# Eight half blocks of early gate/up products for nine, and one more Strassen unit in the FFN

## The chip, the cores and the metric

The kernel runs on one core of a Trainium2 chip. A core has TensorE (PE, matmuls; PEld is its weight load), VectorE (DVE), ScalarE (ACT), GpSimd (POOL), SyncE (SP, which here only issues DMAs) and 16 DMA engines. Engines run their own instruction streams in order and meet through semaphores. The metric is the device time of one execution in microseconds (us); the number for a kernel is the median of several runs.

## The reference

Two parts share one layer-normalised input `xn` (2048 tokens, D = 576): a linear attention with a softmax feature map (32 heads of 18), and a SwiGLU FFN with F = 4608 that gates its output. All numbers are float32.

```python
xn = _layernorm(x)
# attention
q, k, v = split_heads(xn @ wqkv)
pq = einsum("bhsd,hdf->bhsf", q, w_phi)            # same for k
phi_q = concat([softmax(pq), softmax(-pq)])        # same for k
kv = einsum("bhsf,bhsd->bhfd", phi_k, v); z = phi_k.sum(tokens)
o = (phi_q @ kv) / (phi_q @ z + 1e-6)
s = merge_heads(o) @ wo
# FFN
g = silu((silu(xn @ w_gate) * (xn @ w_up)) @ w_down)
return x + s * g
```

## The kernel before, in words

**Precision.** Each float32 operand is split into a high part that TensorE reads exactly (`hi`, a cast on ScalarE) and the rest (`lo`, a subtraction on VectorE), and a product is made of three: hi·hi, hi·lo and lo·hi (`split`, L72). A full product over D = 576 of 128 rows of weights with 512 tokens is 14 matmuls (`xw`, L98).

**Stages.** The attention comes first: layer norm, keys and values, then the 16 q tiles of 128 tokens (`q_tile`, L823). For each pair of q tiles the softmax is done on VectorE (`softmax_parts`, L525: max and min, a subtraction, two exps on ScalarE into two halves of `e`, then the sum; L832 to L842: denominators and scaling of `e`). One pair later `numer` (L845) takes five groups of heads: four transposes into `pt` (L854), cast `ph` and subtraction `pl`, six products with the key-value sums (L861), again cast `oh` and subtraction `ol`; `pt`, `ph` and `pl` have two buffers each. The last group's low part goes through SP (`lo`, `km`). `project` (L872) multiplies with `wo` (14 matmuls for each of four halves, L889), and ScalarE copies the result out (`so` or `e`, L895).

**Early products.** The FFN works on 36 blocks of 128 of F and on two halves of 1024 tokens (i = 0 and 1). For the first blocks the gate and up products are made during the attention (`early_weights`, `early_tile`, L127 and L141): for a half block two token quarters of 512, each 14 matmuls for gate, a silu on ScalarE, 14 matmuls for up, and a product on VectorE; the result `h` goes to DRAM (`h_dram`). `EARLY` = 4 and `FIRST` = (5, 4) say that half 0 has blocks 0 to 4 early and half 1 blocks 0 to 3, nine half blocks. They are written behind the attention in the code, and the scheduler puts their matmuls (`pe`) where the attention leaves PE free. Block 4 of half 0 is the last, written after the rest (L1464 to L1469).

**FFN units.** A later block of a half is a unit of `gate_up` (L1034): gate and up of both quarters in seven products instead of eight (Strassen), 7 matmuls each (`product`, L1010), into `px`, `py`, `pw` and, in the first two units, a `pd` bank. Its weights come from `gate_up_weights` (L958): in half 0, and for blocks under `FIRST[0]` in half 1, from the raw weights `ld`, with four sums on POOL (`ts`, `ld`), four casts, four subtractions (tiles `w`), and a store of the parts in `w_dram` for half 1, which otherwise only loads them. The last 64 of the 576 rows come as "tails" (`wt`), which `tails` (L805) prepares in DRAM during the attention for four blocks at a time: a load, four POOL subtractions, a cast, a subtraction and twelve POOL DMAs. The first units' weights may not start before one of the last projection's copies (L1471, `outs[-3]`).

An early block is in its half a stored unit, which only loads `h`. `units` (L1419) is the order of blocks in each half; stored blocks stand at every fourth place of the beginning, and block 4 of half 1 in the middle. Behind each pair of units the down products (L1136, into `pd`) are queued and drawn a few at a time between the products of the units by `fill` (L1452): four times in a unit of `gate_up`, twice in a stored one.

What sets the order on each engine is the scheduler's list, fixed when the program is built: an instruction that waits holds all behind it on its engine.

Of the kernel before, what the change touches and what calls it, by code (L numbers as in the profile page):

```python
# [23 lines left out]
NF = F // P  # L24
# [5 lines left out]
NL = GROUPS[-1][1]  # L30
NK = NL + NL // 2
QS = 256
EARLY = 4
FIRST = (EARLY + 1, EARLY)
TAILS = (NF - EARLY + 3) // 4
LAG = 3
SHORT = range(22, NF - 5, 4)
# [24 lines left out]
def gated_hedgehog_kernel(ctx: ExitStack, tc, x, w_qk, w_v, consts_in, wo, w_gu, w_tail, w_down, out):  # L62
# [5 lines left out]
    nc = tc.nc  # L68
# [7 lines left out]
    def split_rows(hi, lo, src):  # L76
        nc.scalar.copy(hi, src)
        nc.vector.tensor_sub(lo, src[:, :, 0:2], hi[:, :, 0:2])
        nc.vector.tensor_sub(hi[64:96, :, 2], src[64:96, :, 2], hi[64:96, :, 2])
# [6 lines left out]
    s_dram = dram.tile([S, D], F32, name="s_dram")  # L86
    h_dram = dram.tile([2, FIRST[0], P, HS], F32, name="h_dram")
    x_dram = dram.tile([2, 4, P, 4, P], F32, name="x_dram")
    sum_dram = dram.tile([2, P, 4, 4, 5, P], F32, name="sum_dram")
    w_dram = dram.tile([NF - EARLY, P, 7, 4, P], F32, name="w_dram")  # L90
    t_dram = dram.tile([TAILS, 4, 3, 32, 7, P], F32, name="t_dram")
# [6 lines left out]
    def xw(ps, i, j, cols, wh, wl, stationary_x):  # L98
        pairs = []
        for k in range(2):  # L100
            b = XB[i][2 * j + k]
            for c in range(2):
                pairs += [(b[:, c, cols], w[:, k, c]) for w in (wh, wl)]
                pairs += [(b[:, 3 + c, cols], wh[:, k, c])]
            pairs += [(b[:, 2, cols], wh[:, k, 2])]
        for n, (a, b) in enumerate(pairs):
            l, r = (a, b) if stationary_x else (b, a)
            last = nc.tensor.matmul(ps, l, r, start=n == 0, stop=n == len(pairs) - 1)  # L108
        return last
# [9 lines left out]
    def early_raw_part(f, m):  # L119
        raw = epool.tile([P, 2, 3, P], F32, name="raw", bufs=2)  # L120
        nc.sync.dma_start(raw, w_gu[f, :, m:m + 2])
        return raw

    def early_place():
        return epool.tile([P, 2, 3, P], F32R, name="wh", bufs=3), epool.tile([P, 2, 2, P], F32R, name="wl", bufs=3)

    def early_weights(f, *behind):  # L127
        parts = []
        for m in (0, 2):
            raw = early_raw_part(f, m)  # L130
            parts.append(early_place())
            with ExitStack() as order:
                for b in behind:
                    order.enter_context(tc.issue_after(b.ins))
                with tc.high_priority():
                    split_rows(*parts[-1], raw)
        return parts
# [3 lines left out]
    def early_tile(f, i, parts, js=(0, 1), banks=None, store=nc.sync, behind=None):  # L141
        for j in js:
            pg, pu = banks or [eps.tile([P, BT], F32, name="pe") for _ in range(2)]
            xw(pg, i, j, slice(0, BT), *parts[0], False)
            h = epool.tile([P, BT], F32, name="h")
            with tc.high_priority():
                silus.append(nc.scalar.activation(h, pg, AF.Silu))
            last = xw(pu, i, j, slice(0, BT), *parts[1], False)
            with tc.issue_after(behind.ins) if behind else ExitStack():
                with tc.high_priority():  # L150
                    nc.vector.tensor_mul(h, pu, h)
            store.dma_start(h_dram[i, f, :, j * BT:(j + 1) * BT], h)
        return last

    outs = []
    with ExitStack() as att:
# [18 lines left out]
        with ExitStack() as wst:  # L175
# [4 lines left out]
            with ExitStack() as pst:  # L180
# [15 lines left out]
                xns, ws, wv, halves = {}, {}, {}, {}  # L196
# [485 lines left out]
            order = [6, 7, 0, 1, 2, 3, 4, 5]  # L682
# [101 lines left out]
        with ExitStack() as qst:  # L784
# [113 lines left out]
            order = list(range(S // QS // 2, S // QS)) + list(range(S // QS // 2))  # L898
# [13 lines left out]
                with tc.issue_after(last_e[3 * n // 2 + 2].ins):  # L912
                    tails(n, exps[NT + 3 * n // 2 + 2])

        for f, halves in [(1, (0,)), (0, (0,))] + [(f, (1, 0)) for f in range(2, EARLY)]:
            parts = first_weights.pop() if f == 1 else early_weights(
                f, *{0: read[2 * NT + 1:2 * NT + 2], 2: (read[2 * NT + 3], exps[NT + 1])}.get(f, ()))
            for i in halves:
                early_tile(f, i, parts, (1,) if f == 1 else (0, 1), behind=read[2 * NT + 1] if f == 1 else None)
# [8 lines left out]
    def operands(i):  # L928

        xo = [None] * 7  # L930
        for n in (0, 6, 3, 1, 5, 4, 2):
            if n < 3:
                j = (0, 1, 3)[n]
                if i:
                    t = xpool.tile([P, 5, BT], F32R, name=f"X0{j}")
                    nc.sync.dma_start(t.bitcast(F32), a_dram[n])
                else:
                    t = XB[0][j]
                xo[n] = [t[:, c] for c in range(5)]
                continue  # L940
            j = n - 3
            t = xpool.tile([P, 5, BT], F32R, name=f"X1{j}")
            parts = 1 if i else 4
            rows = t.bitcast(F32).rearrange("p c n -> p (c n)").rearrange("p (a m) -> p a m", a=parts)
            src = sum_dram[i, :, j].rearrange("p s c n -> p (s c n)").rearrange("p (a m) -> p a m", a=parts)
            for a in range(parts):
                nc.sync.dma_start(rows[:, a], src[:, a])
            v = t.rearrange("p c n -> p (c n)").rearrange("p (s c n) -> p s c n", s=4, c=5)
            xo[n] = [v[:, :, c] for c in range(5)]
        return xo  # L950

    def raw_weights(f):
        ld = fw.tile([P, 2, D], F32, name="ld", bufs=2).rearrange("p a b -> p (a b)")
        ld = ld[:, 0:8 * P].rearrange("p (m c n) -> p m c n", m=4, c=2)
        nc.sync.dma_start(ld, w_gu[f, :, :, 0:2])
        return ld

    def gate_up_weights(i, f, ld=None):  # L958

        parts, wt = {}, wts[0]  # L960
        wts.reverse()
        n, q = divmod(f - EARLY, 4)
        raw = i == 0 or f < FIRST[0]
        if raw:
# [3 lines left out]
        def ready(m, src):  # L968
            k = 1 if m == 6 else 2
            w = fw.tile([P, k, 4, P], F32R, name=f"w{k}", bufs=2 if k == 1 else 4)  # L970
            if not raw:
                nc.sync.dma_start(w.bitcast(F32), w_dram[f - EARLY, :, m:m + k])
            else:
                split(w[:, :, 0:2], w[:, :, 2:4], src)
                if i == 0 and f < NF - 1:
                    nc.sync.dma_start(w_dram[f - EARLY, :, m:m + k], w.bitcast(F32))
            for c in range(k):
                parts[m + c] = w[:, c]
# [11 lines left out]
        else:  # L990
            ready(2, ld[:, 2:4] if raw else None)
        held = {0: silus[-2:-1], 2: tops[0:1], 3: tops[1:2]}.get(f - FIRST[0]) if i == 0 else None

        def last(held=held):
            with tc.issue_after(held[0].ins) if held else ExitStack():
                ready(6, ld[:, 1:2] if raw else None)
# [3 lines left out]
        elif i == 0 and f in SHORT:  # L1000
            later.append(lambda: last(copies[-1:]))
        elif (i, f) == (0, FIRST[0] + 3):
            opened.append(lambda: ready(6, ld[:, 1:2]))
# [416 lines left out]
    for i in range(2):  # L1420
        order = [NF - 1] * i + list(range(FIRST[0], NF - i))
        if i:
            order.insert(NF // 2, EARLY)
        for f in range(FIRST[i]):
            order.insert(4 * f + 1 - i, f)
        units += [(i, n, f) for n, f in enumerate(order)]
# [34 lines left out]

    todo = [(i, f) for i, n, f in units if f >= FIRST[i] and (i == 0 or f < NF - 1)]
    kept = []
    parts = early_weights(EARLY)  # L1464
    first_rows = [acc[:, 1].rearrange("p (a b) n -> p a (b n)", a=2)[:, n] for n in range(2)]
    for t, f in zip(first_rows, (FIRST[0], 0)):
        nc.sync.dma_start(t, w_down[f * P:(f + 1) * P, :])
    xo = operands(0)
    early_tile(EARLY, 0, parts, store=nc.gpsimd)  # L1469
    early_raw = [raw_weights(f) for _, f in todo[0:2]]  # L1470
    with tc.issue_after(outs[-3].ins):  # L1471
        ready = [gate_up_weights(*todo.pop(0), early_raw.pop(0))]
# [84 lines left out]
```

## Time and profile before

| | us |
|---|---|
| median of 3 runs | 1579.47 (1579.38 to 1579.89) |
| profiled execution | 1580.98 |
| its span, first to last instruction | 1579.2 |
| attention with the q tiles, from the first early matmul at L108 to the last projection | 219.9 to 456.8 |
| first matmul of the FFN units (L1051) | 467.70 |

The profile is of one execution. A group's row gives the busy time and the mean of one instruction; matmuls overlap in PE's pipeline, so the distance between two starts, not the record's length, tells what one costs. The chain of waits is followed back from the last instruction, so it tells which engine's work sets the end. The rows that matter are shown in the prediction.

### The profile page before, as it was taken

The page shows a single profiled execution, that of the slowest core. Times are in us where ns is not written, and L with a number is a line of the kernel's source. Part 1 is how long each engine was busy: PE and PEld are TensorE (multiplying, and loading weights), DVE is VectorE, ACT ScalarE, POOL GpSimd, SP SyncE. Part 2 cuts the span into 40 slices and gives each one's busy share as a digit, 9 for nine tenths or more (in the row PEclk, how much of TensorE's full clock was granted, in tenths as well). Part 3 has the DMA queues.
Part 4 walks back from the last instruction along what each step waited for, and adds up shares of the span by engine and source line. Part 5 has one row for each costly group of instructions (what it writes and reads, how often), then busy time and mean ns, then how long its engine had stood idle before and what let it go on. Part 6 is the DMA issues. An engine that isn't in the chain of part 4 may idle for free.

```text
span 1579.2 us, 25305 instructions
## 1 busy us (share of the span) xinstructions
PE 1570.4 (99%) x9371; PEld 1415.5 (90%) x9371; DVE 1162.8 (74%) x1722; ACT 729.0 (46%) x1408; POOL 671.5 (43%) x723
## 2 busy tenths in 40 slices
PE   9999999999999999999999999999999999999998
PEld 7999999999988898898888888888888888888887
DVE  7777769999947787987777778545766667666577
ACT  6633344545445644444544444454333343333334
POOL 5766653334125545563644444313323324133133
PEclk9999999999999999999999999999999999999999
DMA  9424343336357455454545543964545655555445
GB/s 284 142 67 165 135 154 117 105 118 209 120 185 259 159 181 198 161 182 174 186 161 202 177 168 125 355 210 139 155 146 157 193 173 161 175 184 187 145 118 182
DMA packets 123287, 269.05 MB, mean 170 GB/s; under 512 B 12436, under 2 KB 54100, under 8 KB 121884
## 3 DMA queue, kind: packets, MB, share of 16 engines
q1 hardware_dynamic: 110572, 246.57, 47.6%
q0 software_dynamic: 3552, 12.59, 2.8%
q10 hardware_dynamic: 9040, 8.28, 1.6%
q8 instruction: 74, 1.21, 0.3%
q14 instruction: 49, 0.40, 0.1%
HBM read 167.54 MB, written 99.09 MB: 169 GB/s over the span
## 4 chain that ended last, share of the span: by engine, by line
PE 96%; POOL 1%; DVE 1%; DMA 1%; issue 1%; ACT 0%; SPq 0%; DVEq 0%; POOLq 0%; ACTq 0%
PE px L1014 25%; PE pd L1136 25%; PE pw L1014 12%; PE p L108 6%; PE py L1014 6%; PE pe L108 5%; PE p L889 4%; PE kvp L547 2%; PE pt L861 2%; PE pe L50 1%; PE vx L636 1%; PE pt L854 1%; PE tp L50 1%; PE vw L636 1%; DMA wst<-in_A_w_qk 0%
## 5 line engine op out<-in xcount | busy, mean ns | idle before, releaser
L1136 PEld LDWEIGHTS pd<-dw,hh 128*128 128x128 f32 x3000 | 421.8, 188 | 19.8 <-DVE acc L1372 0.8
L1136 PE MATMUL pd<-dw,hh 128*128 128x288 f32 x3000 | 435.7, 294 | 0.0
L1014 PE MATMUL px<-X,w 128*128 128x512 f32 x1512 | 385.6, 390 | 0.0
L1014 PEld LDWEIGHTS px<-X,w 128*128 128x128 f32 x1512 | 274.6, 188 | 46.1
L1014 PE MATMUL pw<-X,w 128*128 128x512 f32 x744 | 188.8, 389 | 0.0
L1014 PEld LDWEIGHTS pw<-X,w 128*128 128x128 f32 x744 | 139.5, 188 | 28.9
L1372 DVE TENSOR_TENSOR acc<-pd,acc 128x576 f32<-128x576 f32 x128 | 96.4, 753 | 93.3 <-PE pd L1136 92.6
L1047 DVE TENSOR_TENSOR s<-pw,s 128x512 f32<-128x512 f32 x126 | 86.4, 687 | 89.5 <-ACT s L1042 78.9
L1042 ACT COPY s<-px 128x512 f32<-128x512 f32 x126 | 73.6, 584 | 144.9 <-PE px L1014 144.7
L73 ACT CAST hh<-ha 128x512 fp32r<-128x512 f32 x139 | 82.2, 620 | 94.2 <-PE pd L1136 68.7
L74 DVE TENSOR_TENSOR hh<-ha,hh 128x512 fp32r<-128x512 f32 x139 | 111.8, 829 | 18.8 <-ACT hh L73 18.5
L1344 POOL TENSOR_TENSOR hb<-hb 128x512 f32<-128x512 f32 x34 | 46.6, 1372 | 157.2 <-DVE hb L1059 156.8
L74 DVE TENSOR_TENSOR w<-ld,w 128x512 fp32r<-128x512 f32 (+1 forms) x96 | 76.9, 803 | 38.6 <-ACT w L73 37.7
L1014 PE MATMUL px<-X,wt 128*128 128x512 f32 x252 | 98.0, 389 | 0.0
L1014 PE MATMUL py<-X,w 128*128 128x512 f32 x378 | 96.5, 390 | 0.0
L1357 POOL TENSOR_TENSOR ha<-ha 128x512 f32<-128x512 f32 x34 | 52.3, 1554 | 100.1 <-DVE hh L74 94.7
L1331 POOL TENSOR_TENSOR h<-ha,hb 128x512 f32<-128x512 f32 x34 | 44.5, 1309 | 107.2 <-DVE ha L1063 76.4
L983 POOL TENSOR_TENSOR ts<-ld 128x256 f32<-128x256 f32 x32 | 26.8, 839 | 139.6 <-issue 67.4
L73 ACT CAST w<-ld 128x512 fp32r<-128x512 f32 (+1 forms) x96 | 52.7, 550 | 70.3 <-POOL ld L986 40.6
L1067 ACT COPY py<-px 128x512 f32<-128x512 f32 x63 | 36.0, 572 | 106.1 <-PE px L1014 94.6
L108 PE MATMUL pe<-X,wh 128*128 128x512 f32 x260 | 80.4, 395 | 0.0
L1014 PEld LDWEIGHTS py<-X,w 128*128 128x128 f32 x378 | 68.3, 188 | 10.8
(325 smaller groups left out, 3242.3 us busy)
## 6 DMA issues: line engine op xcount, KB each, us to landing
w_dram<-w SPq DMA_DIRECT2D x90, 512.0 KB, 2.6
w<-w_dram SPq DMA_DIRECT2D x90, 512.0 KB, 4.3
wt<-t_dram SPq DMA_DIRECT2D x62, 336.0 KB, 4.4
ld<-in_B_w_gu SPq DMA_DIRECT2D x32, 512.0 KB, 6.3
rt<-in_B_w_down SPq DMA_DIRECT2D x33, 288.0 KB, 5.1
rb<-in_B_w_down SPq DMA_DIRECT2D x33, 288.0 KB, 3.3
w_dram<-w SPq DMA_DIRECT2D x30, 256.0 KB, 2.1
w<-w_dram SPq DMA_DIRECT2D x30, 256.0 KB, 2.7
```

What stands on the lines that cost most here:

```text
L73: cast = nc.scalar.copy(hi, src)
L74: return cast, nc.vector.tensor_sub(lo, src, hi)
L108: last = nc.tensor.matmul(ps, l, r, start=n == 0, stop=n == len(pairs) - 1)
L889: nc.tensor.matmul(ps[:, 0:HALF], a, bw, start=k == 0, stop=k == len(mm) - 1)
L1014: nc.tensor.matmul(ps, l, r, start=first and n == 0, stop=last and n == len(mm) - 1, skip_group_check=True)
L1042: snaps.append(nc.scalar.copy(t, ps))
L1047: nc.vector.tensor_add(t, ps, t)
L1136: nc.tensor.matmul(ps, l, r, start=first and n == 0 and m == 0, stop=n == len(hs) - 1 and m == 2, skip_group_check=True)
L1331: sub(s, g["h"][0][0], g["h"][0][1])
L1344: nc.gpsimd.tensor_add(a21, a21, g["h"][1][1])
L1357: sub(a12, a12, g["h"][0][0])
L1372: adds.append(nc.vector.tensor_add(a2, pd[:, :, 0:HALF], a2))
```

## The change

`EARLY` becomes 3 and `FIRST` (5, 3). Half 0 keeps blocks 0 to 4 early. Half 1 keeps only 0 to 2; its block 3 becomes a unit of `gate_up` with raw weights, placed in the middle of the half, and block 4 four places behind it. The early list loses one half block of 56 matmuls (block 3, half 1). `TAILS` goes from 8 to 9, as there are now 33 blocks from `EARLY` on.

```diff
-EARLY = 4
-FIRST = (EARLY + 1, EARLY)
+EARLY = 3
+FIRST = (EARLY + 2, EARLY)
 TAILS = (NF - EARLY + 3) // 4
...
-        for f, halves in [(1, (0,)), (0, (0,))] + [(f, (1, 0)) for f in range(2, EARLY)]:
+        for f, halves in [(1, (0,)), (0, (0,))] + [(f, (1, 0)) for f in range(2, EARLY)] + [(EARLY, (0,))]:
...
         if i:
-            order.insert(NF // 2, EARLY)
+            for f in range(EARLY, FIRST[0]):
+                order.insert(NF // 2 + 4 * (f - EARLY), f)
...
-    parts = early_weights(EARLY)
+    parts = early_weights(FIRST[0] - 1)
...
-    early_tile(EARLY, 0, parts, store=nc.gpsimd)
+    early_tile(FIRST[0] - 1, 0, parts, store=nc.gpsimd)
```

The order of instructions moves at the end of the attention. Up to the 14th q tile PE's order is the same. Three places follow, each as it stood before and as it stands now.

The first is ScalarE around the exps of the last q tile (`e`). Before, the table of the silu (L147) is not loaded between the last tile's two exps:

```order
L73 CAST ph<-pt 126x512 x2
L534 ACT_TABLE_LOAD
L534 ACTIVATE e<-e 128x576
L73 CAST oh<-pt 126x256 x2
L73 CAST ph<-pt 126x512
L534 ACTIVATE e<-e 128x576
L73 CAST oh<-pt 126x256
L895 COPY so<-p 128x288
```

Now a silu stands between them, with two table loads, and the copy of a projection too:

```order
L73 CAST ph<-pt 126x512 x2
L73 CAST oh<-pt 126x256 x2
L73 CAST ph<-pt 126x512
L534 ACTIVATE e<-e 128x576
L147 ACT_TABLE_LOAD
L147 ACTIVATE h<-pe 128x512
L73 CAST oh<-pt 126x256
L895 COPY so<-p 128x288
L534 ACT_TABLE_LOAD
L534 ACTIVATE e<-e 128x576
```

The second exp of the last tile moved behind that silu, the copy and both loads.

The second place is PE in the last pair's `numer`, around the products of the first two groups (72 and 126 rows). Before:

```order
L861 MATMUL pt<-ph,KVH 72x256 x2
L861 MATMUL pt<-ph,KVL 72x256 x2
L861 MATMUL pt<-pl,KVH 72x256 x2
L108 MATMUL pe<-X_694,wh 128x512
L108 MATMUL pe<-X_695,wh 128x512
L108 MATMUL pe<-X_695,wl 128x512
L108 MATMUL pe<-X_695,wh 128x512 x2
```

Now, with the end of the last early block (`pe`) in front:

```order
L108 MATMUL pe<-X_695,wl 128x512
L108 MATMUL pe<-X_695,wh 128x512 x2
L854 MATMUL pt<-consts,e 72x128 x3
L854 MATMUL pt<-consts,e 126x128 x3
L861 MATMUL pt<-ph,KVH 72x256 x2
L861 MATMUL pt<-ph,KVL 72x256 x2
L861 MATMUL pt<-pl,KVH 72x256 x2
L861 MATMUL pt<-ph,KVH 126x256 x2
```

All early matmuls now stand ahead of the last tile's transposes, and none between or behind the steps of the last `numer`.

The third is PE at the start of the FFN's units (`w` and `wt` are the weights and their tails, `X` the token sums). Before:

```order
L108 MATMUL pe<-X_695,wl 128x512
L108 MATMUL pe<-X_695,wh 128x512 x2
L1051 MATMUL py<-X_588,w_5275 128x512
L1014 MATMUL px<-X_588,w_5275 128x512 x6
L1014 MATMUL px<-X_588,wt_5162 128x512
L1014 MATMUL pw<-X_5182,w_5284 128x512 x6
L1014 MATMUL pw<-X_5182,wt_5162 128x512
```

Now:

```order
L889 MATMUL p_4548<-WOH,km 128x288
L889 MATMUL p_4548<-WOL,km 128x288
L1051 MATMUL py<-X_588,w_5228 128x512
L1014 MATMUL px<-X_588,w_5228 128x512 x6
L1014 MATMUL pw<-X_5135,w_5237 128x512 x6
L1014 MATMUL pd<-X_5150,w_5241 128x512 x5
L1014 MATMUL px<-X_588,wt_5115 128x512
L1014 MATMUL pw<-X_5135,wt_5115 128x512
```

The units now follow the last projection (L889) at once, and the first three products are begun with all but their tails before the first `wt` is read.

## The prediction

> **What bounds the kernel now.** I read the page's engine shares first, then the chain of work that ended last, then the busy time by stretches.
>
> ```profile
> PE 1570.4 (99%) x9371; PEld 1415.5 (90%) x9371; DVE 1162.8 (74%) x1722; ACT 729.0 (46%) x1408; POOL 671.5 (43%) x723
> PE 96%; POOL 1%; DVE 1%; DMA 1%; issue 1%; ACT 0%; SPq 0%; DVEq 0%; POOLq 0%; ACTq 0%
> 390.00:420.00 30.00, 30.00 (x212) 28.58 (x211) 27.87 (x41) 14.13 (x25) 6.24 (x13) 1.00 0.55 166
> 420.00:450.00 30.00, 30.00 (x199) 26.92 (x198) 22.36 (x41) 14.78 (x27) 0.44 (x1) 1.00 0.23 77
> 450.00:480.00 30.00, 30.00 (x151) 25.50 (x150) 14.64 (x21) 11.43 (x24) 13.79 (x19) 1.00 0.75 253
> 1170.00:1490.00 320.00, 320.00 (x1753) 283.47 (x1753) 208.66 (x300) 119.69 (x236) 100.72 (x84) 1.00 0.56 171
> ```
>
> In the windows the columns are length, busy time of PE, PEld, DVE, ACT and POOL, clock, DMA share and GB/s. TensorE never stops: 96% of the chain is PE, and no stretch quoted shows it idle. So the time is a sum of matmul slots, and any new wait of PE is added in full. But near 400 us VectorE is nearly as full (27.87 of 30). There PE stays busy because early products of the FFN (`pe`) stand between the attention's own. I look for what happens when some are taken out.
>
> The length of a slot comes from runs of equal matmuls in the chain view (start, length, what):
>
> ```profile
> 241.08 13.40 PE pe L108 x59
> 266.18 7.44 PE p L889 x56
> 456.98 10.89 PE pe L108 x48
> 477.61 3.17 PE px L1014 x14
> 437.02 1.04 PE L854 MATMUL pt<-consts,e 128*72 128x128 f32 x8
> 437.82 0.70 PE L108 MATMUL pe<-X,wh 128*128 128x512 f32 x2
> 439.52 0.40 PE L861 MATMUL pt<-ph,KVH 72*72 72x256 f32 x2
> 439.99 0.40 PE L861 MATMUL pt<-pl,KVH 72*72 72x256 f32 x2
> 440.23 0.62 PE L108 MATMUL pe<-X,wh 128*128 128x512 f32 x2
> ```
>
> A 512-wide matmul takes 0.227 us (13.40/59, 10.89/48, 3.17/14), a 288-wide one 0.133 us (7.44/56). The last five rows are of the timeline: eight transposes take 0.1 us each (437.02 to 437.82), six products of L861 0.118 each (439.52 to 440.23). A record's own length overlaps its neighbours and isn't used.
>
> **The count.** One early half block goes: 2 token quarters x gate and up x 14 matmuls = 56, or 12.7 us. It becomes a unit of `gate_up`: 7 products x 7 = 49, or 11.1 us. The down products stay. Net **-1.6 us** (7 x 0.227).
>
> ```profile
> 458.88 0.61 ACT L73 CAST w<-ld 128x512 fp32r<-128x512 f32 x1
> 459.52 0.69 DVE L74 TENSOR_TENSOR w<-ld,w 128x512 fp32r<-128x512 f32 x1 [6.59 <-ACT w L73]
> L816 DVE TENSOR_TENSOR tl<-tl,th x8: 1081/1083/1084, 269.2 to 407.4; 128x896 f32<-128x896 f32 x8
> ```
>
> The new unit stands in the second FFN half, with weights read raw, as block 4 has there already. VectorE is busy 208.66 of 320 us in that stretch and PE 320 of 320, so its casts, subtractions and loads lie beside matmuls. Cost 0; if that cover were gone, four casts of 0.61 and four subtractions of 0.69, 5.2 us.
>
> The ninth tail group costs VectorE and ScalarE one instruction each, POOL four and twelve DMA issues.
> VectorE's 1.1 us stand just before the last softmax sum, where VectorE waits for ScalarE anyway (below). Cost 0, at most 1.1. POOL is busy 0.44 of the 30 us from 420.
>
> **Where the fillers are missing.** PE's order is the same up to the 14th of the 16 q tiles. From the last q tile on, 38 early matmuls are left for 98 before, and none behind the last softmax, where 71 stood. These waits follow.
>
> ```profile
> 418.40 0.39 PE L108 MATMUL pe<-X,wh 128*128 128x512 f32 x1
> 423.21 1.28 ACT L534 ACT_TABLE_LOAD   x1
> 424.51 0.69 ACT L534 ACTIVATE e<-e 128x576 f32<-128x576 f32 x1
> 429.89 1.35 DVE L538 TENSOR_REDUCE sm<-e 128x64 f32<-128x1152 f32 x1
> 432.43 0.40 ACT L895 COPY so<-p 128x288 f32<-128x288 f32 x1 [2.28 <-PE p L889]
> 435.62 1.36 DVE L842 TENSOR_TENSOR e<-e,y 128x1152 f32<-128x1152 f32 x1
> 436.89 0.29 PE L889 MATMUL p<-WOL,km 108*128 108x288 f32 x1
> 445.25 0.37 ACT L73 CAST oh<-pt 126x256 fp32r<-126x256 f32 x1 [1.00 <-PE pt L861]
> 445.65 0.42 DVE L74 TENSOR_TENSOR ol<-pt,oh 126x256 fp32r<-126x256 f32 x1 [0.68 <-ACT oh L73]
> ```
>
> *Last softmax.* Before, PE comes to the last transposes (437.02) just as VectorE ends the scaling of the last e (435.62 + 1.36). Now PE does 15 more early matmuls ahead of that point (4 before the last q product ends, 11 behind), +3.4 us: 440.4. VectorE's side: ScalarE now loads the Silu table, computes a silu, and loads the Exp table back between the two exps of the last tile. The silu needs PE to have gone 24 early matmuls, 24 of L861 and 12 transposes beyond the last q product, which ended at 418.40 (the first `pe` behind it) and now ends 0.9 later, 419.3: 5.4 + 2.8 + 1.2, so 428.7. Behind it stands a copy of `p`, ready after 17 projections: 428.7 + 2 early matmuls (0.5) + 6 of L861 (0.7) + 2.3 + 0.3 (the last one's length) = 432.5. Copy 0.4, table 1.3, exp 0.7: 434.9, and some 0.1 between engines, 435.0. From the sum to the end of the scaling took 436.98 - 429.89 = 7.1 us, with one oh/ol subtraction (0.4) that now comes earlier, so 6.7: 441.7. PE waits 441.7 - 440.4 = **1.3 us**. Bounds: 0, if that tail of ScalarE is quicker by it, and 2.6, two table loads in full.
>
> [...]
>
> *Last head groups.* Behind the transposes each of five groups goes PE, ScalarE cast, VectorE subtraction, PE, cast, subtraction, with two buffers of `pt`.
>
> ```profile
> 438.02 0.58 ACT L73 CAST ph<-pt 72x512 fp32r<-72x512 f32 x1 [0.40 <-PE pt L854]
> 438.63 0.69 DVE L74 TENSOR_TENSOR pl<-pt,ph 72x512 fp32r<-72x512 f32 x1 [1.65 <-ACT ph L73]
> 456.68 0.29 PE L889 MATMUL p<-WOL,km 108*128 108x288 f32 x1
> ```
>
> The stretch from 437.02 to 456.81 is 19.8 us: 20 transposes, 30 of L861, 56 projections and 23 early matmuls make 2.0 + 3.5 + 7.4 + 5.2 = 18.1, so 1.7 us of waiting are there already. Without the 23, and with two transposes done earlier, the work is 12.7. Going through the new order with cast 0.58, subtraction 0.69, short cast 0.37 and short subtraction 0.42, PE waits 1.3 us for the first group, 0.65 for the buffer of the second, 0.4, 0.2 and 0.3 for the next, 0.65 for the last `oh`: 3.5 us. New: 3.5 - 1.7 = **1.8 us**. Bounds: 0, and 5.2 (every early matmul there turned into waiting).
>
> *Opening of the FFN.* Before, 48 early matmuls (10.9 us) cover the splitting of the first weights, which stands behind the last projection's copies on ScalarE. Now the FFN follows at once.
>
> ```profile
> 457.01 0.40 ACT L895 COPY e<-p 128x288 f32<-128x288 f32 x1 [1.37 <-PE p L889]
> 457.44 0.36 ACTq L896 DMA_DIRECT2D s_dram<-e  x1
> 460.61 0.43 SPq L981 DMA_DIRECT2D wt<-t_dram  x1
> 467.70 0.39 PE L1051 MATMUL py<-X,w 128*128 128x512 f32 x1
> wt<-t_dram SPq DMA_DIRECT2D x62, 336.0 KB, 4.4
> rt<-in_B_w_down SPq DMA_DIRECT2D x33, 288.0 KB, 5.1
> ld<-in_B_w_gu SPq DMA_DIRECT2D x32, 512.0 KB, 6.3
> ```
>
> Let E be the end of the projections (456.81 before). The copy starts at E+0.2, its DMA is issued by E+1.0, the cast of `w` ends at E+1.6, and the first matmul comes at E+1.7: wait 1.7. The low part ends at E+2.35, 0.3 after PE wants it. Then 18 matmuls run to E+6.1. The tail rows `wt` are issued 0.4 behind the low part and land 4.4 us later, E+7.15: wait 1.0. The copy of `px` stands on ScalarE behind a cast of `dw`, whose rows (issued E+0.25, 5.1 to land) and POOL's work on them hold it to about E+8.5, 0.3 beyond PE. A table load (1.28) ahead of the first silu makes about 0.2 more. Sum **3.5 us**. Bounds: 1.7 (the cast alone) and 10.9 (nothing starts earlier than now). I keep near the rows of the chain, since each link has one.
>
> Sum: -1.6 + 1.3 + 1.8 + 3.5 = **+5.0 us**. On the profiled execution (1580.98, span 1579.2) that is 1586.0, span 1584.2; on the median of the runs, 1579.47, it is **1584.5 us**, 0.3% slower. 0.2% (3.2 us) is about what a measurement of this kernel can tell from no change.
>
> **Rivals.** (1) *Not slower, small waits.* PE and VectorE are level at 436.9 now; if ScalarE fits its table loads into the 3.4 us by which PE comes later, the softmax wait is 0, and the chain behind it then runs on free engines. With 0, 0.5 and 2.5: +1.4, 1580.9. It decides at waits of 4.8 us in all, below which the change can't be told from none. For it: ACT is half idle there (14.78 of 30). Against: the order of ACT is fixed, and each of its links has a row.
> (2) *The count alone:* no wait, 1577.9. Against: the first cast can't start before the projections' copies end.
> (3) *Queue heads.* On SP the load of the third weights (`ld`, 6.3 us) now stands behind the stores of the second unit's parts. The last of these needs a buffer that PE frees with the first unit's `py` group (E+8.5 and 14 matmuls, E+11.7), then a cast and a subtraction (1.3) and its stores: the load goes at about E+13.8 and lands at E+20; ScalarE's cast waiting for it blocks copies that release PE, which wants them from E+21 on. If it, or the `dw` rows, land 3 us later: 1587.5.
> (4) *The clock.* The first matmuls run slower:
>
> ```profile
> 1.00 3.60 PE L169 MATMUL fp<-idle 128*128 128x512 bf16 x8 [1.00 <-POOL least L189]
> 9.74 1.57 PE L50 MATMUL fp<-PHI,wst 126*128 126x126 f32 x12 [1.24 <-DMA wst<-in_A_w_qk]
> ```
>
> Eight took 3.60 us, slots of 0.43. After a wait of 1.24 us slots are short (12 in 1.57). If the opening's wait were 1.7 longer and brought such a slow start, 3.6 us at half rate, lost 1.9: +3.6, 1588.1. Nothing quoted shows a drop inside the program; the clock is 1.00 throughout.
>
> [...]
>
> **How the numbers follow.** Forecast 0.55 (own range 1582.7 to 1586.5), small waits 0.20, count alone 0.05, queue heads 0.16, clock 0.04. Slower: 0.55 + 0.16 + 0.04 = 0.75. The other 0.25 are within 0.2%, but for 0.02 faster, if the second half gained too. The range 1580.8 to 1588.2 leaves out the count, the later part of the queue case and a bit of the small waits, under 2 in 10; the bounds added up (0 to some 17) are wider, but no row makes several extremes meet.
>
> **What would show it.** PE's waits over 0.2 us, now nearly all at the program's start: some 1.3 us ahead of the last transposes behind DVE L842, some 3.5 in the groups behind, and 1.7 and 1.0 at L1051 and at the first `wt`, released by ACT and by a DMA; 49 more matmuls at L1014 and 56 fewer into `pe`. The last projection should end near 458, the first L1051 near 460, not 467.70. The forecast is wrong if PE shows under 4.8 us of new waits, or if more waits appear in the second FFN half, for which I count none.

## The result: 1.3% slower, four times the forecast loss

| | us |
|---|---|
| changed kernel, median of 4 runs | 1601.24 (1599.29 to 1601.71) |
| kernel before, beside it, median of 4 | 1579.68 (1579.38 to 1583.2) |
| ratio | 1.0129, 95% interval 1.0111 to 1.0147 |
| span of the profiled execution, before and after | 1579.2 and 1599.6 |

The forecast was 1584.5 us, with a range to 1588.2. The sign was right, the size was not: +21.6 us for +5.0. First the page of the changed kernel, engine shares and chain:

```profile
PE 1576.7 (99%) x9364; PEld 1417.9 (89%) x9364; DVE 1174.4 (73%) x1729; ACT 736.6 (46%) x1418; POOL 687.3 (43%) x743
PE 91%; DVE 3%; POOL 2%; ACT 2%; issue 1%; DMA 1%; SPq 0%; DVEq 0%; ACTq 0%; POOLq 0%
```

There are seven matmuls fewer, and the chain is 91% PE for 96%. Then its list of what PE waited for (sum, times, longest):

```profile
PE px L1014 <- ACT s L1042: 7.0, 3, 2.4
PE py L1051 <- ACT w L73: 1.5, 1, 1.5
PE pd L1136 <- DVE hh L74: 1.5, 1, 1.5
PE px L1014 <- DMA wt<-t_dram: 1.3, 1, 1.3
PE pt L861 <- DVE pl L74: 1.3, 2, 1.1
PE pt L854 <- DVE e L842: 1.1, 1, 1.1
```

The forecast had the second, fourth, fifth and sixth of these waits. The largest is px behind ScalarE's copy `s`, three times: the one in the opening it had only as a rival, the two in the second half not at all. The windows (columns as before) show where, and a second loss, in the clock column:

```profile
420.00:450.00 30.00, 27.75 (x177) 24.81 (x176) 22.85 (x39) 13.43 (x25) 5.77 (x12) 0.94 0.34 102
450.00:480.00 30.00, 25.77 (x129) 20.44 (x128) 15.32 (x21) 13.28 (x26) 11.86 (x14) 1.00 0.68 237
480.00:500.00 20.00, 17.33 (x82) 13.66 (x80) 17.10 (x19) 9.95 (x20) 15.30 (x15) 1.00 0.67 227
500.00:520.00 20.00, 18.91 (x91) 16.55 (x92) 14.34 (x19) 12.01 (x24) 10.94 (x11) 0.91 0.64 231
1170.00:1490.00 320.00, 315.18 (x1713) 278.54 (x1712) 205.40 (x295) 118.08 (x233) 100.76 (x85) 0.99 0.54 163
```

Before, PE was busy 30 of 30 and 320 of 320 us here, at a clock of 1.00. A ledger of the lost time comes from the starts of all matmuls: the distance to the next start less the slot of that width (0.227 us for 512, 0.132 for 288, and so on), summed. A stretch at half clock (0.50 in the clock column) is 3.41 us long here and so costs 1.7.

| us lost beyond the slots | before | after | new | forecast |
|---|---|---|---|---|
| slots (9371 and 9364 matmuls) | | | -1.6 | -1.6 |
| end of the attention, 420 to the last projection | 1.7 | 7.3 | +5.6, of it 1.7 half clock | +3.1 |
| opening, last projection to 520 | 0.2 | 11.2 | +11.0, of it 1.7 half clock | +3.5 |
| second half, from 1200 | 0.7 | 7.8 | +7.0, of it 1.7 half clock | 0 |
| elsewhere | 11.2 | 9.9 | -1.3 | 0 |

The sum, +20.7, is the difference of the spans (20.4) within 0.3. Of the -1.3 elsewhere, 0.9 lie in the program's first 20 us.

**The second half.** The timelines around its first wait, of SP, POOL, ScalarE and PE (start, length, what, and in brackets the idle time before and its releaser):

```profile
1304.28 0.34 SPq L1122 DMA_DIRECT2D out<-ts  x1
1306.62 1.02 POOL L983 TENSOR_TENSOR ts<-ld 128x256 f32<-128x256 f32 x1 [4.42 <-DVE sx L1372]
1308.82 0.62 ACT L73 CAST w<-ts 128x512 fp32r<-128x512 f32 x1 [1.67 <-POOL ts L984]
1310.86 0.41 ACT L73 CAST w<-ld 128x256 fp32r<-128x256 f32 x1 [1.42 <-POOL ld L986]
1312.19 0.58 ACT L1042 COPY s<-px 128x512 f32<-128x512 f32 x1
1312.82 1.65 PE L1014 MATMUL px<-X,w 128*128 128x512 f32 x6 [2.41 <-ACT s L1042]
```

Read it upwards. PE waits for a copy of `px` that stands on ScalarE behind two casts of the next unit's weights. They wait for POOL's sums in the tile `ts`. POOL's first sum starts only when the finished rows of `late_finish`, which uses the same one-buffer tile, have left it (issued 1304.28, POOL at 1306.62; the releaser named, VectorE at 1306.4, writes another tile, so that it is `ts` is read from the code here, and tested below). The same happens at 1379.5.

**The opening.** SP's timeline, of the kernel before and then of the changed one: weight stores (L976), raw weights `ld` (L955), rows of the down weights (L1305):

```profile
468.61 1.79 SPq L955 DMA_DIRECT2D ld<-in_B_w_gu  x1
474.20 1.75 SPq L976 DMA_DIRECT2D w_dram<-w  x2
476.04 0.41 SPq L1305 DMA_DIRECT2D rb<-in_B_w_down  x1
```

```profile
474.44 0.75 SPq L955 DMA_DIRECT2D ld<-in_B_w_gu  x1
481.66 5.98 SPq L976 DMA_DIRECT2D w_dram<-w  x4
487.74 0.42 SPq L1305 DMA_DIRECT2D rb<-in_B_w_down  x1
```

Although PE reaches the opening earlier, `ld` is issued 5.8 us later and `rb` 11.7 us later: `ld` now stands behind two stores more than before, `rb` behind four, which are those of one unit, and these stores wait for VectorE's low parts. What follows, on the changed kernel's POOL, ScalarE and PE:

```profile
492.24 1.25 POOL L1332 TENSOR_TENSOR td<-rb,rt 128x288 f32<-128x288 f32 x1
497.13 0.73 POOL L983 TENSOR_TENSOR ts<-ld 128x256 f32<-128x256 f32 x1
498.81 0.62 ACT L73 CAST w<-ts 128x512 fp32r<-128x512 f32 x1 [0.65 <-POOL ts L984]
500.46 0.58 ACT L1042 COPY s<-px 128x512 f32<-128x512 f32 x1
501.10 2.13 PE L1014 MATMUL px<-X,w 128*128 128x512 f32 x6 [2.22 <-ACT s L1042]
```

The sums of `td` wait for `rb`, the sums of `ts` stand behind them, and the copy that PE wants stands on ScalarE behind the cast of `ts`. In the kernel before `td` began at 479.69.

### The profile page after: what moved, and what is told of

The parts are those of the page before. It is cut to its first block, busy times and chain, and to the rows that moved or that the text cites. A ratio compares the mean times of both kernels' runs of the same rounds, so it can differ in the third digit from the quotient of the medians.

```text
span 1599.6 us, 25341 instructions
## 1 busy us (share of the span) xinstructions
PE 1576.7 (99%) x9364; PEld 1417.9 (89%) x9364; DVE 1174.4 (73%) x1729; ACT 736.6 (46%) x1418; POOL 687.3 (43%) x743
## 4 chain that ended last, share of the span: by engine, by line
PE 91%; DVE 3%; POOL 2%; ACT 2%; issue 1%; DMA 1%; SPq 0%; DVEq 0%; ACTq 0%; POOLq 0%
PE px L1014 24%; PE pd L1136 24%; PE pw L1014 12%; PE p L108 6%; PE py L1014 6%; PE pe L108 4%; PE p L889 3%; PE kvp L547 2%; PE pt L861 2%; PE pe L50 1%; PE vx L636 1%; PE pt L854 1%; PE tp L50 1%; PE vw L636 1%; PE vy L636 0%
## 5 line engine op out<-in xcount | busy, mean ns | idle before, releaser
L1136 PEld LDWEIGHTS pd<-dw,hh 128*128 128x128 f32 x3000 | 423.8, 189 | 21.7 <-DVE hh L74 1.7
L1136 PE MATMUL pd<-dw,hh 128*128 128x288 f32 x3000 | 437.7, 295 | 1.5 <-DVE hh L74 1.5
L1014 PE MATMUL px<-X,w 128*128 128x512 f32 x1536 | 394.3, 391 | 7.4 <-ACT s L1042 7.0
L1014 PEld LDWEIGHTS px<-X,w 128*128 128x128 f32 x1536 | 279.3, 188 | 56.5 <-ACT s L1042 8.6
L1014 PE MATMUL pw<-X,w 128*128 128x512 f32 x756 | 192.0, 389 | 0.0
L1047 DVE TENSOR_TENSOR s<-pw,s 128x512 f32<-128x512 f32 x128 | 87.7, 686 | 92.6 <-ACT s L1042 82.0
L74 DVE TENSOR_TENSOR hh<-ha,hh 128x512 fp32r<-128x512 f32 x139 | 110.7, 821 | 20.3 <-ACT hh L73 20.2
L1344 POOL TENSOR_TENSOR hb<-hb 128x512 f32<-128x512 f32 x34 | 47.1, 1385 | 155.9 <-DVE hb L1059 155.6
L74 DVE TENSOR_TENSOR w<-ld,w 128x512 fp32r<-128x512 f32 (+1 forms) x99 | 81.9, 830 | 36.0 <-ACT w L73 35.2
L1372 DVE TENSOR_TENSOR X<-pd,X 128x576 f32<-128x576 f32 x64 | 48.2, 754 | 27.9 <-PE pd L1136 27.3
```

Source lines behind the costliest of these rows:

```text
L74: return cast, nc.vector.tensor_sub(lo, src, hi)
L1014: nc.tensor.matmul(ps, l, r, start=first and n == 0, stop=last and n == len(mm) - 1, skip_group_check=True)
L1047: nc.vector.tensor_add(t, ps, t)
L1136: nc.tensor.matmul(ps, l, r, start=first and n == 0 and m == 0, stop=n == len(hs) - 1 and m == 2, skip_group_check=True)
L1344: nc.gpsimd.tensor_add(a21, a21, g["h"][1][1])
L1372: adds.append(nc.vector.tensor_add(a2, pd[:, :, 0:HALF], a2))
```

## Experiments

Two theories run through them. A: PE waits where the early matmuls are missing, since VectorE, ScalarE and POOL can't go faster. C: the order on SP (loads behind stores) sets the opening's later waits. Others are named where they come up. All times stand beside runs of the kernel before on the same chip, 1580.2 to 1580.6 us.

**1. Places of the two units (e1_even), and late_finish (e4_skip_rows).**

```diff
-                order.insert(NF // 2 + 4 * (f - EARLY), f)
+                order.insert(NF // 2 + 1 + 4 * (f - EARLY), f)
```

> The two units with raw weights stand one place later in half 1 (places 22 and 26 for 21 and 25 of 36). Theory A: in the changed kernel the POOL sums of these units (L983, into ts) wait until the finished rows of late_finish have left the same tile ts, and the casts of ts and ld stand on ScalarE ahead of the copy (L1042) that PE waits for; the preparation of a unit at an even place begins before that call of late_finish, so both waits of 2.57 us go, and with them the half-clock stretch of 1.69 us behind the second: 1601.2 - 6.8 = 1594.4 us. Rival B: the waits come from the unit itself, whose product groups px, pw, py, px follow each other without down products between: they stay, 1601.2 us.

```diff
-        if i and n >= 15 and late:
+        if i and n >= 15 and late and n not in (19, 23):
```

> The changed kernel, with late_finish not called behind places 19 and 23 of half 1, the ones just ahead of the two units with raw weights (its calls come later in the half). Theory A (tile ts held by late_finish): both waits of 2.57 us go, 1594.4 us, though the units stay at the odd places 21 and 25. Rival B (the odd place, or a unit without down products between its groups): they stay, 1601.2 us.

Measured: 1594.15 us (ratio 1.0088, 1.0071 to 1.0104) and 1592.81 us (one run). Both lose nothing in the second half any more. The windows from 1170 to 1490, first of e1_even, then of e4_skip_rows:

```profile
1170.00:1490.00 320.00, 320.00 (x1749) 283.19 (x1748) 209.96 (x303) 121.77 (x240) 99.51 (x86) 1.00 0.55 167
```

```profile
1170.00:1490.00 320.00, 320.00 (x1748) 283.12 (x1747) 206.20 (x299) 121.91 (x241) 99.17 (x86) 1.00 0.54 162
```

In e4_skip_rows the units stay at the odd places, and the waits still go: it is `late_finish` just ahead of them. (Rival B's reason was not there: in the changed kernel the wait comes in the unit before the new one, and the new one has down products, L1136 at 1324.06 and 1328.82, between its groups.) Without that call POOL makes the first sum in `ts` at 1273.10 instead of 1306.62, which is what a shared tile would do; `late_finish`'s other work went with it, so the tile is not tested apart. e1_even came as forecast, but not for the reason given: its sum begins no earlier (1306.95). ScalarE's cast of `ts` stands there only at 1323.77, 16.8 us behind the sum's start, where the changed kernel has 2.2 us, so the late sum holds nobody. Block 4's unit in the kernel before stood at an even place (22).

**2. Cover without the saving (e2_keep), the saving without the unit (e3_no_unit).**

The list of early blocks (only its end is shown):

```diff
-[(f, (1, 0)) for f in range(2, EARLY)] + [(EARLY, (0,))]
+[(f, (1, 0)) for f in range(2, EARLY + 1)]
```

> The early half block of block 3, half 1, is computed as before (56 matmuls, 12.7 us) and its result is not used; the unit in the FFN stays where the change put it. Theory A: the waits at the end of the attention and at the opening of the FFN (5.6 and 11.0 us more than before, 3.4 of it at half clock) are there because these 56 matmuls no longer cover the chain of VectorE, ScalarE and POOL: both nearly vanish, 1601.2 + 12.7 - 16.6 = 1597.3 us, with the two waits of 2.57 us in the second half kept. Rival B: the opening's waits come from the queues and the longer list of tail groups: 11.0 us stay, 1608.3 us.

In the kernel before, for e3_no_unit (again the end of the list):

```diff
-[(f, (1, 0)) for f in range(2, EARLY)]
+[(f, (1, 0)) for f in range(2, EARLY - 1)] + [(EARLY - 1, (0,))]
...
-        h = stored(h_dram[i, f], fill) if f < FIRST[i] else ...
+        h = stored(h_dram[i, 2 if (i, f) == (1, 3) else f], fill) if f < FIRST[i] else ...
```

> The kernel before without the early half block of block 3, half 1 (56 matmuls fewer); no unit takes its place: half 1 reads the stored h of block 2 for block 3, so that block's gate and up products for half 1 are left out. Theory A: all waits of the attention's end and the opening are as in the changed kernel, and none is in the second half: 1601.2 - 11.1 (49 matmuls) - 7.0 = 1583.1 us, more than the kernel before although it does 12.7 us less of matmuls. Rival B: part of the opening's waits comes with the ninth tail group and the shifted list of units: 1575 to 1580 us.

Measured: 1607.42 and 1583.48 us, one run each. e3_no_unit came as theory A says: it has 56 matmuls (12.7 us) less than the kernel before, and it is 3.3 us slower. e2_keep did not. The end of the attention was as before (1.5 us lost), but the opening lost 9.6 us with all its cover, near rival B (1608.3). So something else in the change costs the opening as much.

**3. The ninth tail group alone (b_tails9),** on the kernel before:

```diff
-TAILS = (NF - EARLY + 3) // 4
+TAILS = 9
...
     tail = laid["B_w_gu"][EARLY:, 0:32, :, 2]
+    tail = np.concatenate([tail, tail[:4]])
```

> The kernel before with nine tail groups for eight (TAILS = 9; the ninth repeats the first four blocks and is not read), nothing else. Theory E: the ninth group changes the scheduler's order on SP at the opening of the FFN: the third ld and the second pair's rb fall behind the weight stores of two more units, as in e2_keep, and the waits of e2_keep's opening come back (9.6 us in 460 to 520, 1.7 of it at half clock): 1580 + 9.4 = 1589 us. Rival F (the prediction's price): the group costs its own instructions only, 0 to 1.1 us: 1579.5 to 1581 us.

Measured: 1590.05 us, ratio 1.0060 (1.0045 to 1.0075). SP's timeline of it, and its longest wait on PE:

```profile
470.26 6.42 SPq L976 DMA_DIRECT2D w_dram<-w  x3
476.77 0.55 SPq L955 DMA_DIRECT2D ld<-in_B_w_gu  x1
...
483.35 6.94 SPq L976 DMA_DIRECT2D w_dram<-w  x4
490.38 0.41 SPq L1305 DMA_DIRECT2D rb<-in_B_w_down  x1
...
506.19 2.23 PE L1014 MATMUL px<-X,w 128*128 128x512 f32 x6 [4.35 <-ACT s L1042]
```

A tail group that nobody reads, prepared during the attention, costs 9.4 us, as theory E forecast. Its instructions are not the price: the end of the attention loses no more than before. The scheduler, which fixes all orders when the program is built, puts SP's queue at the opening in another order. e3_no_unit has eight groups and that order too (`rb` at 488.94, behind four stores), so the missing half block brings it about by itself as well.

**4. What in the opening waits for what (e5 to e8),** all on e1_even (1594.15 us, 9.7 us lost in the opening).

```diff
 def down_rows(f, name):
     t = fq.tile([P, D], F32, name=name, bufs=2)
-    nc.sync.dma_start(t, w_down[f * P:(f + 1) * P, :])
+    with tc.high_priority():
+        nc.sync.dma_start(t, w_down[f * P:(f + 1) * P, :])
```

> The units at the even places as in e1_even (1594.15 us), and the rows of the down weights (rt, rb; L1305) loaded with high priority, so that on SP they stand ahead of the first units' weight stores (L976). Theory C: at the opening the second pair's rb stands on SP behind four stores of the third unit's weights that wait for VectorE; POOL's sums of td wait for rb, its sums ts of the next unit for those, ScalarE's cast of ts holds the copy s, and PE waits 2.4 us at px near 499. With rb early this wait goes: 1591.7 us; the wait of 1.6 us for the low part hh near 492 stays, since it is VectorE's own backlog. Rival A: VectorE is the bound of the whole opening, and the wait at px only moves: 1594 us.

```diff
-                if i == 0 and f < NF - 1:
+                if i == 0 and FIRST[0] + 3 <= f < NF - 1:
...
-    nc.sync.dma_start(w.bitcast(F32), w_dram[f - EARLY, :, m:m + k])
+    nc.sync.dma_start(w.bitcast(F32), w_dram[max(f, FIRST[0] + 3) - EARLY, :, m:m + k])
```

> e1_even without the stores to w_dram of the first three units of half 0 (blocks 5 to 7): nothing is left on SP that holds the loads ld and rb; half 1 reads block 8's weights for blocks 5 to 7 in place of their own. Theory C (loads behind stores): the wait of 2.4 us at px near 499 goes, 1591.7 us, the other waits of the opening stay. If the transfers of the stores slow the loads or the engines as well, the waits of 1.6 us at wt and at hh shrink too: down to 1588.5 us. Rival A (VectorE bound): 1594 us.

```diff
-early_tile(FIRST[0] - 1, 0, parts, store=nc.gpsimd)
+early_tile(FIRST[0] - 1, 0, parts, (0,), store=nc.gpsimd)
+with tc.issue_after(lasts[-1].ins):
+    early_tile(FIRST[0] - 1, 0, parts, (1,), store=nc.gpsimd)
```

(`lasts` holds the projections' matmuls.)

> e1_even with the last early half block's second token quarter (28 early matmuls, 6.4 us, its silu and its product) held behind the last projection. Theory A (the waits are where the early matmuls are missing, and the cover can be moved): the opening's waits fall by 6.4 us; at the attention's end PE has 6.4 us less to do ahead of the last transposes, but that silu and its two table loads (3.2 us) leave ScalarE's chain of the last softmax, so the wait there grows by 3.2 us only: 1594.15 - 3.2 = 1591.0 us. Rival D (cover only moves, nothing is gained): 1594 us. Rival C (the opening's later waits are set by SP's order, not by the start): the wait at px stays, 1594 to 1596 us.

```diff
+        skip = first and i == 0
...
         def p7(g):
             B11, B12, B21, B22 = blocks(g)
+            if skip:
+                return g["h"][0][1], B12
```

(and likewise in p4, p5, p6 and p3)

> e1_even without POOL's sums for the first four pairs of Strassen's down products in half 0 (L1331 to L1349: h, td, rt, hb, ha); the products take the unsummed tiles. Theory A (VectorE's backlog, made by POOL at work beside it: the same subtraction of 128x512 takes 0.69 us alone and 1.0 to 1.8 us between 480 and 500): VectorE's times there fall to about 0.7 us, and both the wait for hh (1.6) and the one at px (2.4) go: 1590.1 us. Rival C (SP's order): the px wait goes, since POOL's queue no longer waits for rb, but the wait for hh stays: 1591.7 us.

| | us | opening lost | of it half clock |
|---|---|---|---|
| e5_rows_first | 1593.88 (ratio 1.0084, 1.0064 to 1.0104) | 9.3 | 0 |
| e6_no_stores | 1593.65, one run | 8.8 | 3.4 |
| e7_pin28 | 1597.46 (1.0106, 1.0089 to 1.0123) | 9.4 | 1.7 |
| e8_no_pool | 1590.53, one run | 5.7 | 0 |

**e5** and **e6** missed theory C's 1591.7 us and came out at rival A's 1594; which of the two holds is read from the traces. In e5 the wait near 499 went, and one of 2.2 us came at 486.7, since the third `ld` still stood behind the stores: moving `rb` alone is not enough. In e6, without the stores, nothing is lost between 480 and 500 (0.07 us, 5.1 in e1_even), as theory C says. That the time is no better comes from the first 15 us: with waits of 1.7, 1.6 and 1.9 us there, 6.8 us ran at half clock (the run's mean granted clock is 0.996, for 0.998 in e1_even), a loss e1_even's opening didn't have.

**e7** missed all three forecasts. 28 matmuls held back as cover left the wait of 2.4 us at px (503.2), and the attention's end lost 12.0 us for 7.8 (1.7 of the rise is a second stretch at half clock). Here, cover moved from one thin place to another gained nothing.

**e8**, one run, came near theory A's 1590.1 us: the waits for `hh` went and the one at px fell to 1.1 us, where A had it go. The subtraction for `hh` (L74) in the changed kernel, and beside POOL's sum (L1344) another VectorE instruction (L1047) that reads PSUM; then `hh` in e8_no_pool:

```profile
491.07 1.76 DVE L74 TENSOR_TENSOR hh<-ha,hh 128x512 fp32r<-128x512 f32 x1
509.14 1.30 POOL L1344 TENSOR_TENSOR hb<-hb 128x512 f32<-128x512 f32 x1 [4.93 <-DVE hb L1059]
509.34 0.69 DVE L1047 TENSOR_TENSOR s<-pw,s 128x512 f32<-128x512 f32 x1 [0.28 <-PE pw L1014]
509.95 1.04 DVE L74 TENSOR_TENSOR hh<-hb,hh 128x512 fp32r<-128x512 f32 x1
```

```profile
488.24 0.68 DVE L74 TENSOR_TENSOR hh<-ha,hh 128x512 fp32r<-128x512 f32 x1
```

With POOL at rest it takes 0.68 us, beside POOL's sums up to 1.76. So both theories hold in part: SP's order decides when POOL's sums come, and when they come late they also fall on VectorE's backlog.

**5. The loads put ahead of the stores (e9, e10, e13).** In the loop over the units, on e1_even (e9) and on e2_keep with the even places (e10):

```diff
+                if i == 0 and n < 4:
+                    early_raw.append(raw_weights(todo[1][1]))
                 ready.append(gate_up_weights(*todo.pop(0), *early_raw[0:1]))
-                early_raw = []
+                early_raw = early_raw[1:]
...
+    rows2 = [down_rows(units[n][2], name) for n, name in ((2, "rt"), (3, "rb"))]
```

> e1_even (1594.15 us) with the same loads ahead of the stores; the early matmuls stay as the change left them. Theory C: the waits at hh and px between 480 and 505 (5.2 us in e1_even) go, those for the first cast, the first wt and the py copy (3.8 us) stay: 1589 us. Rival A (the whole side chain of the opening is late, since nothing in it starts earlier): the waits only move, 1594 us.

> e2_keep (all nine early half blocks) with the two units at even places, and with the loads ld of the third to fifth unit and rt, rb of the second pair issued ahead of the stores of the unit before, so that SP's order at the opening is near the kernel before's. Theory C (the waits of e2_keep's opening are loads behind stores on SP): with cover and order both as before only the 49 matmuls of the added unit are left, 1580 + 11.1 = 1591 us. Rival A (VectorE bound, or the ninth tail group in another way): only the 7.0 us of the second half go, 1600.4 us.

Measured: e9 took 1589.31 us (1.0054, 1.0039 to 1.0069), as theory C forecast; its opening loses 5.6 us, of it 1.0 past 480, with no wait there over 0.4. e10 took 1601.55 us (1.0132, 1.0115 to 1.0149), a miss by 10 us. It is close to rival A's 1600.4, but the old waits were gone, and a new one stood at the first sum. POOL's and PE's timelines of e10_keep_ahead:

```profile
471.76 0.55 POOL L152 DMA_DIRECT2D h_dram<-h  x1 [1.99 <-DVE dw L74]
478.59 0.79 POOL L1334 TENSOR_TENSOR td<-acc 128x288 f32<-128x288 f32 x1 [6.28 <-DMA wt<-t_dram]
480.89 1.65 PE L1014 MATMUL px<-X,w 128*128 128x512 f32 x3 [6.67 <-ACT s L1042]
```

The account taken for this is that `rt` and `rb`, loaded early, had shifted `td` in memory onto the last early half block's `h`, whose store (issued at 471.76) has to land first; the profile names another DMA, that of `wt`. e13_keep_ahead3 lays `td` out where it was and also issues `rt` and `rb` only after the first unit, so it does not tell the two apart:

> e10_keep_ahead again, with the tile td of the first pair laid where it was: in e10 the loads issued early had moved td onto the memory of the last early half block's h, and POOL waited 6.3 us for that h's store. All nine early half blocks, the units at even places, loads ahead of stores. Theory C: with cover and SP's order as in the kernel before only the 49 matmuls of the added unit are left: 1580.5 + 11.1 = 1591.6 us, without a wait over 0.8 us after 460. Rival A: the waits of e2_keep's opening (9.6 us) stay in another place, 1600 us.

Measured: 1592.50 us (1.0076, 1.0058 to 1.0094) for 1591.6. PE's list of waits, without the one at the program's start, has nothing over 0.5 us, and on SP the third `ld` and the second pair's `rb` are issued near their old times (468.61 and 476.04):

```profile
PE px L1014 <- ACT s L1042: 0.5, 1, 0.5
467.36 1.04 SPq L955 DMA_DIRECT2D ld<-in_B_w_gu  x1
478.18 0.59 SPq L1305 DMA_DIRECT2D rb<-in_B_w_down  x1
```

With cover as before and the order near it, the change costs 12.0 us: the added unit's 49 matmuls (11.1 us) and little else.

**6. The table loads at the last softmax (e14_silu_late),** on e9:

```diff
+            with tc.issue_after(exps[-1].ins) if f == FIRST[0] - 1 else ExitStack():
                 with tc.high_priority():
                     silus.append(nc.scalar.activation(h, pg, AF.Silu))
```

> e9_loads_ahead (1589.31 us) with the two silus of the last early half block held behind the last exp of the attention, so that no table load stands between the last tile's two exps. Theory G (the prediction's step on the last softmax): ScalarE's chain is shorter by two table loads and a silu (3.2 us), PE's wait of 1.28 us ahead of the last transposes goes: 1588.0 us, and 1586.3 us if the half-clock stretch behind it (1.7 us) goes too. Rival H: the silus held back keep the two banks of pe, PE's early matmuls can't run ahead of the last softmax, and the wait is as long or longer: 1589 to 1594 us.

Measured: 1586.29 us (1.0038, 1.0023 to 1.0052), the number that theory G with the clock gave. VectorE's last scaling of `e` in the changed kernel, then in e14_silu_late (where lines stand one lower), with PE's last transposes:

```profile
439.64 1.36 DVE L842 TENSOR_TENSOR e<-e,y 128x1152 f32<-128x1152 f32 x1
441.05 0.85 PE L854 MATMUL pt<-consts,e 128*72 128x128 f32 x6 [1.11 <-DVE e L842]
```

```profile
437.04 1.36 DVE L843 TENSOR_TENSOR e<-e,y 128x1152 f32<-128x1152 f32 x1
438.71 0.82 PE L855 MATMUL pt<-consts,e 128*72 128x128 f32 x6
```

The scaling ends 2.6 us earlier (2.9 against e9, where it starts at 439.96) and PE does not wait. Not all of the gain is the table loads': the held silus also left some early matmuls behind the softmax, where they cover the groups, and brought a new wait of 1.5 us at 425.3. The attention's end loses 4.0 us less than in e9 and the rest 1.2 us more, most of it at the program's start, so it is in part luck that the time agrees so well. This is the best version that keeps the change, and still 5.8 us behind the kernel before: 5.7 us are lost in the opening and 3.6 at the attention's end, where the kernel before loses 1.9 in both together, for 1.6 us of matmuls saved.

## Why the prediction was right in sign and wrong in size

- **The count, -1.6:** right. There are seven matmuls fewer, and e13, 12.0 us behind the kernel before, leaves 0.9 us beside the unit's 11.1.
- **Last softmax, +1.3:** right. The wait was 1.27 us behind L842, by the chain forecast: the silu and both table loads stand between the exps, and PE's end and VectorE's both came some 0.7 us earlier than worked out (439.8 and 441.0 for 440.4 and 441.7). In e14, without them, the wait is gone. (In the changed kernel both loads took 1.28 us, at 428.24 and 432.23, and the silu and the exp behind them began 1.29 us after their load, at 429.53 and 433.52.)
- **Last head groups, +1.8:** +2.6 without the clock (7.3 - 1.3 - 1.7, less 1.7 before). The mechanism was right, the term mis-sized by 0.8.
- **Opening, +3.5:** the links up to the first `wt` were right (1.70 for 1.7, 1.42 for 1.0, 0.47 for 0.3). The step that failed is that the walk stopped there: 9.3 us without the clock, over half of it past 480, one unit beyond. What the runs showed in its place is loads behind stores on SP (`rb` 11.7 us late), POOL's sums behind them and VectorE's low parts late: waits of 1.6 us at 491 and 2.4 at 499. In e9, with the loads ahead, 1.0 us is left of all losses past 480. Rival 3 had this mechanism, loads behind stores with ScalarE's cast blocking copies, at 3 us and 0.16. It deserved the place of the forecast: the order on SP was known, and it shows `rb` behind four more stores.
- **The second half, 0:** wrong by 7.0. "Beside matmuls" was read from engine shares, and block 4's unit was taken as the precedent. It stood at an even place, where the cast of `ts` came 17.4 us behind the sum (1293.36 and 1310.78); the prediction didn't ask how late that sum may come at the new, odd place, nor that `late_finish` uses `ts` just ahead of it. e1 and e4 show it. Waits in the second half were the prediction's own sign of being wrong.
- **The ninth tail group, 0 (at most 1.1):** wrong, +9.4 by itself (b_tails9). It was priced by its instructions, when its price was the new order of other instructions. In the changed kernel it can't be told apart from the missing half block, which brings the same order, so the two don't add up.
- **The clock:** three stretches at half clock, 5.1 us together, for a rival at 0.04 that needed a longer wait than any forecast. The prediction leaned on a trace whose longest shown wait was 1.24 us.

The range failed with the terms. The opening's upper bound, 10.9 ("nothing starts earlier than now"), was nearly met (9.3, and 11.0 with the clock); it had been set aside because several extremes would have to meet. Even the bounds added up, some 17, were passed, since the second half and the clock were not among them.

## What to carry to other kernels

Where a scheduler fixes the order, price an edit by the new order of every queue, the DMA queue first, and follow it until the old and the new order agree again, not until the first waits are explained. A unit that is moved brings its tiles along: look up who else uses each single-buffered tile at the new place. When early work covers a stretch, what it covers is the slowest of all side chains, so the bound "nothing else starts earlier" is the first estimate, to be argued down, not an extreme.

## What the runs showed of the hardware

**The clock fell on a grid, not by the length of a wait alone.** Between the first 4 us and the last 2 us the changed kernel has three half-clock stretches. They begin at 444.04, 502.06 and 1382.70 and are 3.41 or 3.42 us long; the second and third begin 17 and 258 times 3.413 us after the one before. The windows of that grid, with PE's busy time in the second column and the clock in the third from the right:

```profile
440.62:444.04 3.42, 1.92 (x15) 1.69 (x16) 2.26 (x4) 1.18 (x3) 0.56 (x1) 1.00 0.20 77
444.04:447.45 3.41, 3.34 (x16) 3.04 (x15) 1.45 (x3) 1.56 (x4) 0.00 (x0) 0.50 0.08 22
498.65:502.06 3.41, 1.19 (x6) 0.84 (x5) 3.14 (x4) 3.20 (x7) 3.33 (x4) 1.00 0.56 228
502.06:505.48 3.42, 3.42 (x13) 3.06 (x13) 3.42 (x5) 1.72 (x4) 2.07 (x3) 0.50 0.97 335
1311.02:1314.44 3.42, 1.62 (x7) 1.36 (x8) 2.15 (x4) 1.75 (x4) 0.00 (x0) 1.00 0.42 109
1379.29:1382.70 3.41, 1.00 (x6) 0.71 (x5) 2.13 (x5) 1.91 (x4) 0.88 (x1) 1.00 0.32 89
1382.70:1386.12 3.42, 3.42 (x12) 2.89 (x11) 0.70 (x2) 0.59 (x1) 0.00 (x0) 0.50 0.56 173
```

The waits at 1310 and 1380 are equal (2.57 us). The second lies within one window, and the next window runs at half clock. The first is cut by a window's edge at 1311.02, and no half clock follows. PE was idle for 2.22 and 2.41 us of the windows from 498.65 and 1379.29, which half clock followed, and for 1.80 us of that from 1311.02, which it did not. At the last transposes half clock followed a window (440.62) with 1.50 us idle. In e1_even the wait at px (2.2 us in its list) brought none: the clock is 1.00 from 460 to 520. So of the changed kernel's three longest waits, 2.4 to 2.6 us each, two cost 1.7 us more than themselves.

**VectorE beside POOL.** In the changed kernel the subtraction for `hh`, with both inputs in SBUF, took at most 0.70 us in the 152 cases with no POOL instruction beside it, and 0.88 to 1.76 us in the nine that lay wholly beside POOL's. The addition with an input from PSUM (L1047) lay wholly beside POOL's in 53 of 130 cases and never took over 0.69.
